# Scores and V of two units in every second turn, with V's last keys in column pairs

## The chip, the cores and the metric

The kernel runs on one core of a Trainium2 chip. A core has a matrix engine (TensorE) with its own weight loads, a vector engine (VectorE), a scalar engine (ScalarE), a general engine (GpSimd), and queues that issue transfers (here nearly all on SP). Each engine works through its own instructions in order; semaphores tie them together. The metric is the device time of one execution in microseconds, and fewer are better. Products land in PSUM[...]; everything else is in SBUF.

## The reference: what is computed

Two stages follow each other, all in fp32. The first is attention that keeps, for each query, the keys with the 32 highest scores. The second is a gated feed-forward block on the heads put side by side.

```
q, k, v: (8 batches, 8 heads, 576 positions, 64)
scores = (q @ k^T) / 8
kth    = the 32nd largest score of each query
scores = scores where scores >= kth, else -1e9
attn   = exp(scores - max);  attn = attn / (sum(attn) + 1e-9)
x      = (attn @ v), heads side by side: (4608 tokens, 512)
g      = x @ w_gate;  val = x @ w_val             (512 -> 1536)
out    = (g * sigmoid(g) * val) @ w_out           (1536 -> 512)
```

## The kernel before

**Units.** The attention is cut into 160 units, listed in `units`: for each batch, for each of five blocks of queries (`qt` 0 to 4), for each of four pairs of heads (`hp` 0 to 3). The first four query blocks have 128 queries; a unit of them handles both heads with 128 queries on the partitions. The fifth block (`qt == J`) has the last 64 queries, and its unit puts the two heads above each other on the partitions: "one-head" units, with half the work for VectorE. 576 keys are four chunks of 128 and a last one of 64.

**Steps of a unit.** `load` brings k and q in (six transfers on the queue of SP), `prep` transposes them on TensorE into a slab with the 64 features on the partitions, one head in each half. `scores` multiplies: each head uses one half of the rows, so the products are 64*128 tiles (64*64 for one-head units), in four PSUM banks (two), which ScalarE copies to `sc`. `select` finds the 32 highest per query on VectorE, in four rounds of the eight largest (line 328) and three replacements (line 332), and ends with a comparison (line 338). `penalize` adds on GpSimd (line 350). `weigh` takes exponentials and their sums on ScalarE (lines 359 and 364). `normalize` takes the reciprocal on VectorE (line 371) and scales on ScalarE (line 374). `turn` transposes the weights on TensorE (line 386) into `et`, copied by ScalarE (line 387). `values` multiplies V with `et`: for two-head units first the last 64 keys of both heads at once with `vlast`, a 128x128 block-diagonal weight (line 406), and then the four chunks of 128 keys with 64 columns for each head (line 415), which are 128*64 tiles: two heads side by side in the array's columns. For one-head units line 415 has chunks of 64 columns and then 64*64 tiles for the last keys. ScalarE copies the result to `xT` (line 430); where the unit's queries cross a border between blocks of 256 tokens, in two copies.

**Feed-forward.** `feed` does one block of 256 tokens in pieces, as soon as `xT` has all its heads: twelve gate and value products (line 470, full 128*128 tiles, eight instructions a piece), activations on ScalarE and products on GpSimd, and then the output product by seven quarters (line 556). A quantity `credit` meters how many pieces stand in a turn: `share` gives what VectorE's turn has room for, less what scores (0.7), V (0.7) and transposes (0.6) of that turn take on TensorE.

**Order.** The program is written out by hand, one turn per unit, and every engine keeps the order in which the instructions are issued. Turn n holds `select(n)` on VectorE, `penalize(n - 1)` on GpSimd, the scaling of unit n - 2, V of unit n - 3, the scores of unit n + 1, `weigh(n - 1)`, two feed-forward pieces, the transposes of unit n - 2, more pieces with `fetch(n + 2)` among them (which prepares a unit's slab, or issues the load for the next batch), and the reciprocal of unit n - 1 behind `select(n)`. The loads of units 2 and 3 are issued in turns 0 and 1.

**Buffers.** PSUM: five banks of tag `t` rotate through the kq transposes, scores, weight transposes and V; three of tag `f` serve the feed-forward part. SBUF: three buffers each for `sc` and `e`, two for `et` and for raw k and q, four for slabs and for V.

**Weights.** In the first turns the feed-forward weights are loaded and rounded, with work on ScalarE, VectorE and GpSimd (`rounded`, lines 106 to 123); `early` is the part of it that is issued between V and `weigh`.

Of the kernel before, what the change touches and what calls it, by code (L numbers as in the profile page):

```python
# [15 lines left out]
P = 128  # L16
# [9 lines left out]
def kernel(  # L26
# [370 lines left out]
    def values(n):  # L397

        b, qt, hp = units[n]
        vt, v_last, vl = vs[b * NHP + hp]  # L400
        et = state.pop(n)["et"]
        last = qt == J
        ql = R if last else P
        av = ps_t.tile([P, P], FP32, tag="t", name="av")
        if not last:
            nc.tensor.matmul(av[:], vl[:], et[:, J, :], start=True, stop=False)  # L406
        for c in range(J + 1 if last else J):
            kl = R if c == J else P
            for hh in range(2):
                moving = (  # L410
                    et[0:kl, c, hh * R : (hh + 1) * R]
                    if last
                    else et[:, c + hh * (J + 1), :]
                )
                nc.tensor.matmul(  # L415
                    av[hh * R : (hh + 1) * R, 0:ql],
                    v_last[:, hh, :] if c == J else vt[:, hh, c, :],
                    moving,
                    start=last and c == 0,
                    stop=c == (J if last else J - 1),  # L420
                )
        c0 = b * S + qt * P
        at = c0
        while at < c0 + ql:
            kb = at // BLK
            n_c = min((kb + 1) * BLK, c0 + ql) - at
            if kb not in xT:
# [3 lines left out]
                xT[kb][:, hp, at - kb * BLK : at - kb * BLK + n_c],  # L431
                av[:, at - c0 : at - c0 + n_c],
            )
            done[kb] += n_c
# [253 lines left out]
    def share(n):  # L688


        others = 0.0
        for m, cost in ((n + 1, 0.7), (n - TURN, 0.6), (n - VALUES, 0.7)):
            if m >= 0:
                others += cost * (0.5 if units[m][1] == J else 1)
        if units[n + 2][1] == 0:
            others += 0.6

        beside = 6.4 if T[1] else 7.0
        return beside * n_heads(units[n][1]) / 2 - others

# [9 lines left out]
    def finish_unit(n):  # L710
        values(n)
        b, qt, hp = units[n]
        if qt == J and b + 1 < B:
            load_v((b + 1) * NHP + hp)
# [7 lines left out]
    run(fetch(1))  # L722
    credit = [0.0]
    no = iter(())
    scaled = no
    TURN, VALUES = 2, 3
    due = [2.0]
    for n in range(NU + VALUES):
# [3 lines left out]
        nxt = scores(n + 1) if n + 1 < NU else no  # L732
        ahead = fetch(n + 2) if n + 2 < NU else no
# [19 lines left out]
        if n >= VALUES:  # L753
# [80 lines left out]
```

## Time and profile before

| what | value |
|---|---|
| median of three runs | 1810.51 us (1810.4 to 1811.54) |
| the profiled execution | 1810.53 us, of which 1808.5 us from first to last instruction |
| TensorE, products busy | 1703.6 us, 94% of the span |
| TensorE, weight loads busy | 1402.5 us, 78% |
| VectorE busy | 1615.7 us, 89% |
| ScalarE busy | 1221.0 us, 68% |
| GpSimd busy | 1039.2 us, 57% |
| DMA queue of SP and ScalarE | 57.37 MB, 12.3% of 16 engines' span |
| mean granted TensorE clock | 0.965 |

Busy time is the union of an engine's instructions in the profile. A matrix product is issued as two instructions, and consecutive ones overlap in the array; their ends are modelled, so the distance between starts says more than the durations. In the rows of the timeline an "x16" is a run of sixteen such instructions, with the time of the first start and the busy time of the run. A note in brackets is the idle time of the engine just before, and the instruction elsewhere that ended it. In the first 150 us TensorE is busy for 23 to 35 us of each 50 and its clock is granted at 0.59 to 0.73; from 350 us on it is at full clock nearly throughout.

### The profile page before, as it was taken

Reading aid. Unit: us, or ns where it says so; the run is one execution under the profiler, and the core shown is the slowest. Engines: PE = TensorE matmul, PEld = TensorE weight load, DVE = VectorE, ACT = ScalarE, POOL = GpSimd, SP = SyncE. Lnnn points to the kernel's source line nnn. Section 1 sums busy time; section 2 is a strip of 40 time slices with the busy share of each in tenths; the row PEclk is TensorE's granted clock in tenths of the full one; section 3 lists DMA queues with packets and bytes.
Section 4 is the critical chain, followed back from the end, with each engine's and each line's share of the span. In section 5 each row is a group of like instructions: output and inputs, shape, how many; then the busy total and the mean of one; then the engine's idle time right before and its main releaser. Section 6 shows DMA issues by size and latency. Waiting matters only on the chain.

```text
span 1808.5 us, 30379 instructions
## 1 busy us (share of the span) xinstructions
PE 1703.6 (94%) x10756; PEld 1402.5 (78%) x10756; DVE 1615.7 (89%) x3372; ACT 1221.0 (68%) x2977; POOL 1039.2 (57%) x930
## 2 busy tenths in 40 slices
PE   4559999799999999999999999999999999999999
PEld 2337678687888778887888878888888878888877
DVE  7999999999999999998999989998999979999400
ACT  7779676676767676767766776766776667676522
POOL 5778665455564646564555646655556544646434
PEclk7559999999999999999999999999999999999989
DMA  7433030002100030001200021000300011000000
GB/s 191 126 106 93 21 86 1 13 2 48 46 13 1 15 73 8 13 1 27 69 13 1 14 62 32 1 13 4 92 1 13 1 41 28 13 1 13 1 12 12
DMA packets 109304, 59.64 MB, mean 33 GB/s; under 512 B 88544, under 2 KB 96992, under 8 KB 109152
## 3 DMA queue, kind: packets, MB, share of 16 engines
q1 hardware_dynamic: 108016, 57.37, 12.3%
q8 instruction: 85, 1.39, 0.3%
q14 instruction: 67, 0.55, 0.1%
q10 hardware_dynamic: 1136, 0.33, 0.1%
HBM read 48.23 MB, written 9.44 MB: 32 GB/s over the span
## 4 chain that ended last, share of the span: by engine, by line
PE 83%; DVE 8%; ACT 6%; POOL 2%; issue 0%; DMA 0%; SPq 0%; ACTq 0%; POOLq 0%
PE f L470 40%; PE x_ps L556 9%; PE av L415 8%; PE s L308 7%; PE y_ps L556 7%; PE etps L386 6%; DVE m L328 3%; DVE e L332 3%; PE s L294 2%; PE av L406 2%; ACT et L387 1%; PE o_ps L516 1%; ACT e L359 1%; DVE e L338 1%; DVE size L121 1%; ACT kqT L268 1%
## 5 line engine op out<-in xcount | busy, mean ns | idle before, releaser
L328 DVE MAX8 m<-e 128x8 f32<-128x576 f32 x864 | 614.1, 746 | 3.3
L350 POOL TENSOR_TENSOR e<-e,sc 128x1152 f32<-128x1152 f32 (+1 forms) x160 | 383.0, 2394 | 86.1 <-DVE tot L371 70.1
L332 DVE MATCH_REPLACE8 e<-m,e 128x576 f32<-128x576 f32 x576 | 423.1, 740 | 0.0
L470 PE MATMUL f<-xT,wg 128*128 128x256 f32 x1728 | 406.5, 383 | 0.6 <-ACT xT L430 0.6
L470 PE MATMUL f<-xT,wv 128*128 128x256 f32 x1728 | 403.4, 382 | 0.0
L470 PEld LDWEIGHTS f<-xT,wg 128*128 128x128 f32 x1728 | 321.6, 191 | 61.0 <-issue 19.8
L470 PEld LDWEIGHTS f<-xT,wv 128*128 128x128 f32 x1728 | 320.6, 190 | 59.3 <-issue 19.7
L498 POOL TENSOR_TENSOR h<-h,half_g 128x512 f32<-128x512 f32 x108 | 137.7, 1275 | 285.5 <-ACT h L497 267.8
L503 POOL TENSOR_TENSOR h<-h,val 128x512 f32<-128x512 f32 x108 | 139.6, 1293 | 190.7 <-ACT val L502 190.4
L359 ACT ACTIVATE e<-e,bias 128x576 f32<-128x576 f32 x288 | 224.7, 795 | 26.7 <-POOL e L350 26.5
L374 ACT ACTIVATE e<-e,tot 128x576 f32<-128x576 f32 x288 | 210.1, 776 | 27.6 <-DVE tot L371 27.5
L387 ACT COPY et<-etps 128x512 f32<-128x512 f32 (+1 forms) x448 | 182.4, 480 | 53.6 <-PE etps L386 52.8
L332 DVE MATCH_REPLACE8 e<-m,sc 128x576 f32<-128x576 f32 x288 | 211.5, 739 | 0.0
L328 DVE MAX8 m<-sc 128x8 f32<-128x576 f32 x288 | 202.5, 738 | 9.3 <-ACT sc L313 9.3
L386 PE MATMUL etps<-ident,e 128*128 128x128 f32 (+1 forms) x1312 | 175.9, 279 | 18.7 <-ACT xT L430 12.7
L386 PEld LDWEIGHTS etps<-ident,e 128*128 128x128 f32 (+1 forms) x1312 | 155.9, 144 | 42.7 <-issue 25.2
L313 ACT COPY sc<-s 128x288 f32<-128x288 f32 x512 | 167.6, 417 | 26.5 <-PE s L308 25.3
L308 PE MATMUL s<-kqT 64*128 64x288 f32 x1024 | 170.3, 454 | 15.9 <-ACT kqT L268 15.1
L338 DVE TENSOR_SCALAR e<-sc,m 128x576 f32<-128x576 f32 x288 | 179.6, 659 | 1.1
L415 PE MATMUL av<-et,v 128*64 128x128 f32 (+1 forms) x2560 | 173.6, 280 | 6.9 <-ACT et L387 6.9
L415 PEld LDWEIGHTS av<-et,v 128*64 128x64 f32 x2560 | 136.4, 144 | 32.1 <-ACT et L387 9.3
L495 ACT ACTIVATE h<-f 128x512 f32<-128x512 f32 x108 | 64.1, 593 | 128.2 <-PE f L470 128.1
(73 smaller groups left out, 2038.8 us busy)
## 6 DMA issues: line engine op xcount, KB each, us to landing
v<-in_v_dram SPq DMA_DIRECT2D x32, 256.0 KB, 3.1
kq_in<-in_k_dram SPq DMA_DIRECT2D x63, 128.0 KB, 3.0
kq_in<-in_q_dram SPq DMA_DIRECT2D x63, 128.0 KB, 3.1
w<-in_moe_w_gate_dram SPq DMA_DIRECT2D x12, 512.0 KB, 3.8
w<-in_moe_w_val_dram SPq DMA_DIRECT2D x12, 512.0 KB, 3.8
w<-in_moe_w_out_dram SPq DMA_DIRECT2D x12, 512.0 KB, 3.6
out_dram<-o SPq DMA_DIRECT2D x38, 128.0 KB, 2.4
out_dram<-o SPq DMA_DIRECT2D x16, 256.0 KB, 2.4
```

What stands on the lines that cost most here:

```text
L308: nc.tensor.matmul(ps[:, 0:half], slab[d, q0 : q0 + P], slab[d, k0 : k0 + half])
L328: nc.vector.max(m[:, t, 8 * r : 8 * r + 8], cur[:, hs])
L332: nc.vector.match_replace(e[:, hs], m[:, t, 8 * r : 8 * r + 8], cur[:, hs], LOWEST)
L338: nc.vector.tensor_scalar(e[:, hs], sc[:, hs], m[:, t, TOP_K - 1 : TOP_K], FAR, ALU.is_lt, ALU.mult)
L350: nc.gpsimd.tensor_tensor(e[:, every], e[:, every], sc[:, every], ALU.add)
L359: nc.scalar.activation(e[:, hs], e[:, hs], AF.Exp, bias=bias[:, t : t + 1], scale=scale, accum_out=tot[:, t : t + 1],)
L374: nc.scalar.mul(e[:, hs], e[:, hs], tot[:, t : t + 1])
L386: nc.tensor.transpose(ps[0:kl, c * P : (c + 1) * P], e[:, k0 : k0 + kl], ident[:])
L387: nc.scalar.copy(et[0:kl, c0 : c0 + cn, :], ps[0:kl, 0 : cn * P].rearrange("p (c j) -> p c j", c=cn),)
L415: nc.tensor.matmul(av[hh * R : (hh + 1) * R, 0:ql], v_last[:, hh, :] if c == J else vt[:, hh, c, :], moving, start=last and c == 0, stop=c ...
L470: nc.tensor.matmul(ps[:, i, :], w[:, kc, m * P : (m + 1) * P], x[:, kc, :], start=(kc == 0), stop=(kc == KC - 1),)
L556: nc.tensor.matmul(ps, lhsT, T[i][m], start=m == 0, stop=m == MQ - 1)
```

## The change

Work is regrouped, and nothing of the result changes.

- In an even turn n the scores of units n + 1 and n + 2 are made, and V of units n - 4 and n - 3, in this order on TensorE: first scores, V of both, second scores. An odd turn has neither. The first turns (0 and 1) make one unit's scores each.
- On ScalarE the copies of the first scores stand before the V copy; the copies of the second scores stand behind `weigh(n - 1)`.
- The last 64 keys of a two-head unit go through two 128x64 halves of the same block-diagonal weight, as column tiles, in place of one 128x128 product.
- Both V results lie in one PSUM bank and are copied to `xT` by one instruction (two where a block border is crossed).
- `share` counts the costs in the turns in which they now fall. `fetch` runs one unit further ahead, and the loads of units 2 and 3 are issued before the first turn and in turn 0.

```diff
--- before.py
+++ after.py
@@ -394,33 +394,39 @@
 
     xT, done = {}, {}
 
-    def values(n):
-
-        b, qt, hp = units[n]
-        vt, v_last, vl = vs[b * NHP + hp]
-        et = state.pop(n)["et"]
+    def values(ns):
+
+        b, qt, hp0 = units[ns[0]]
         last = qt == J
         ql = R if last else P
-        av = ps_t.tile([P, P], FP32, tag="t", name="av")
-        if not last:
-            nc.tensor.matmul(av[:], vl[:], et[:, J, :], start=True, stop=False)
-        for c in range(J + 1 if last else J):
-            kl = R if c == J else P
-            for hh in range(2):
-                moving = (
-                    et[0:kl, c, hh * R : (hh + 1) * R]
-                    if last
-                    else et[:, c + hh * (J + 1), :]
-                )
-                nc.tensor.matmul(
-                    av[hh * R : (hh + 1) * R, 0:ql],
-                    v_last[:, hh, :] if c == J else vt[:, hh, c, :],
-                    moving,
-                    start=last and c == 0,
-                    stop=c == (J if last else J - 1),
-                )
+        av = ps_t.tile([P, 2, P], FP32, tag="t", name="av")
+        for i, n in enumerate(ns):
+            assert units[n] == (b, qt, hp0 + i)
+            vt, v_last, vl = vs[b * NHP + hp0 + i]
+            et = state.pop(n)["et"]
+            for c in (*range(J), J) if last else (J, *range(J)):
+                kl = R if last and c == J else P
+                for hh in range(2):
+                    d = slice(hh * R, (hh + 1) * R)
+                    if c == J:
+                        weights_, at = (v_last[:, hh, :], d) if last else (vl[:, d], None)
+                    else:
+                        weights_, at = vt[:, hh, c, :], d if last else None
+                    moving = (
+                        et[0:kl, c, at]
+                        if last
+                        else et[:, c + (0 if c == J else hh * (J + 1)), :]
+                    )
+                    nc.tensor.matmul(
+                        av[d, i, 0:ql],
+                        weights_,
+                        moving,
+                        start=c == (0 if last else J),
+                        stop=c == (J if last else J - 1),
+                    )
         c0 = b * S + qt * P
         at = c0
+        hps = slice(hp0, hp0 + len(ns))
         while at < c0 + ql:
             kb = at // BLK
             n_c = min((kb + 1) * BLK, c0 + ql) - at
@@ -428,10 +434,10 @@
                 xT[kb] = ffn.tile([P, NHP, BLK], FP32, tag="xT", name="xT", bufs=3)
                 done[kb] = 0
             nc.scalar.copy(
-                xT[kb][:, hp, at - kb * BLK : at - kb * BLK + n_c],
-                av[:, at - c0 : at - c0 + n_c],
+                xT[kb][:, hps, at - kb * BLK : at - kb * BLK + n_c],
+                av[:, 0 : len(ns), at - c0 : at - c0 + n_c],
             )
-            done[kb] += n_c
+            done[kb] += n_c * len(ns)
             at += n_c
 
     def store(o, g0, cols=slice(0, DM), queues=(nc.sync,)):
@@ -689,14 +695,25 @@
 
 
         others = 0.0
-        for m, cost in ((n + 1, 0.7), (n - TURN, 0.6), (n - VALUES, 0.7)):
+        costs = [(m, 0.7) for m in scored(n) + valued(n)] + [(n - TURN, 0.6)]
+        for m, cost in costs:
             if m >= 0:
                 others += cost * (0.5 if units[m][1] == J else 1)
-        if units[n + 2][1] == 0:
+        if units[n + 3][1] == 0:
             others += 0.6
 
         beside = 6.4 if T[1] else 7.0
         return beside * n_heads(units[n][1]) / 2 - others
+
+    def scored(n):
+
+        ahead = [n + 1] if n < 2 else [] if n % 2 else [n + 1, n + 2]
+        return [m for m in ahead if m < NU]
+
+    def valued(n):
+
+        behind = [] if n % 2 else [n - 4, n - 3]
+        return [m for m in behind if 0 <= m < NU]
 
     def pieces(n):
         for _ in range(n):
@@ -707,11 +724,12 @@
         for _ in steps:
             pass
 
-    def finish_unit(n):
-        values(n)
-        b, qt, hp = units[n]
-        if qt == J and b + 1 < B:
-            load_v((b + 1) * NHP + hp)
+    def finish_units(ns):
+        values(ns)
+        for n in ns:
+            b, qt, hp = units[n]
+            if qt == J and b + 1 < B:
+                load_v((b + 1) * NHP + hp)
 
     load(0)
     rounding(2)
@@ -720,17 +738,18 @@
     run(scores(0))
     early[0]()
     run(fetch(1))
+    load(2)
     credit = [0.0]
     no = iter(())
     scaled = no
-    TURN, VALUES = 2, 3
+    TURN = 2
     due = [2.0]
-    for n in range(NU + VALUES):
+    for n in range(NU + 3):
         nh = n_heads(units[n][1]) if n < NU else 1
         topk = select(n) if n < NU else no
         norm = normalize(n - 1) if 0 <= n - 1 < NU else no
-        nxt = scores(n + 1) if n + 1 < NU else no
-        ahead = fetch(n + 2) if n + 2 < NU else no
+        nxt = [scores(m) for m in scored(n)]
+        ahead = fetch(n + 3 if n else 2) if n + 3 < NU else no
 
         def dve(k, beside=True):
 
@@ -750,17 +769,24 @@
             penalize(n - 1)
         flush(on_pool)
         run(scaled)
-        if n >= VALUES:
-            finish_unit(n - VALUES)
-        run(nxt)
+        if nxt:
+            run(nxt.pop(0))
+        if valued(n):
+            finish_units(valued(n))
+        if nxt:
+            next(nxt[0])
         early[0]()
         if 0 <= n - 1 < NU:
             weigh(n - 1)
+        if nxt:
+            run(nxt.pop())
 
 
         dve(2, beside=False)
-        if 2 <= n + 2 < NHP:
-            load(n + 2)
+        if n == 0:
+            run(ahead)
+            load(3)
+            ahead = fetch(3)
         if n < NHP:
             load_v(n)
         pieces(2)
```

## The prediction

> **What bounds the kernel now.** I read the page first: TensorE's products are busy 1703.6 of 1808.5 us, its weight loads 1402.5, VectorE 1615.7, and the chain that ended last is 83% TensorE and 8% VectorE. The Trainium skill, "Perfetto Trace Analysis", Identifying the Most-Contended Engine, warns that busy time of products says little; so next the stages. One long window over the steady part, from 350 to 1650 us (columns: span, then busy time of TensorE, its loads, VectorE, ScalarE, GpSimd, then clock):
>
> ```profile
> 350.00:1650.00 1300.00, 1283.97 (x8338) 1071.43 (x8337) 1236.90 (x2601) 901.67 (x2235) 727.22 (x661) 1.00 0.09 22
> ```
>
> TensorE is idle 16.0 us of 1300, VectorE 63.1. Then TensorE's timeline through one turn (start, busy, instructions):
>
> ```profile
> 960.27 3.62 PE L470 MATMUL f<-xT,wv 128*128 128x256 f32 x16
> 963.73 0.38 PE L406 MATMUL av<-et,vlast 128*128 128x128 f32 x2
> 964.04 1.09 PE L415 MATMUL av<-et,v 128*64 128x128 f32 x16
> 965.07 1.24 PE L308 MATMUL s<-kqT 64*128 64x288 f32 x8
> 966.24 3.72 PE L470 MATMUL f<-xT,wg 128*128 128x256 f32 x16
> 969.79 1.15 PE L386 MATMUL etps<-ident,e 128*128 128x128 f32 x9
> ```
>
> There is no gap: every group starts where the one before ends. Only start-to-start times count, since ends are modelled. And VectorE at the end of that turn (in brackets the idle time and who ended it):
>
> ```profile
> 969.14 0.17 DVE L371 RECIPROCAL tot<-tot 128x2 f32<-128x2 f32 x1 [1.07 <-ACT tot L364]
> 970.98 0.09 DVE L332 MATCH_VALUE_LOAD e<-m,sc 128x8 f32 x1 [0.35 <-PE etps L386]
> ```
>
> VectorE waits for what follows TensorE. Taking the distance between reciprocals over the whole trace, an undisturbed two-head turn of VectorE is 10.56 us and a one-head turn 6.2 to 6.3; TensorE's turn is 10.5 with four feed-forward pieces and 12.2 with five; the five from 951.50 to 1008.34 average 11.37. From about 300 us on the time is TensorE's. Before that, and in the first 190 us above all, VectorE has no idle time and TensorE plenty: nothing is gained there. After the last softmax a whole feed-forward block (1743 to 1808 us) remains, which the change leaves alone. Where the 16 us of idle time sit: in the one-head turns at each batch's end, by the waits
>
> ```profile
> 1050.04 0.49 PE L406 MATMUL av<-et,vlast 128*128 128x128 f32 x2 [1.35 <-ACT et L387]
> ```
>
> **What the skill says.** "TensorEngine Tiling (Array Packing)", Key Properties: a change of tiling mode, not just of tile, drains the array. "TensorE: Matmul & The Clock Gate", Part 3, The mechanism: a weight load overlaps running products only where it goes to other rows. The trace agrees. A 256-column instruction goes every 0.216 us (3.46 for sixteen, 960.27 to 963.73), so 128 columns cost 0.108, and 288 columns 0.243. Pairs of column tiles and of row tiles run together. Over this, entering column tiles costs 0.31 - 2 x 0.108 = 0.10; entering row tiles 1.03 - 8 x 0.108 = 0.17; going back to the full array 1.17 - 4 x 0.243 = 0.20, and then 3.55 - 3.46 = 0.09 for the first loads. Going into the transposes costs nothing of this kind (nine in 0.99). So a turn pays 0.10 + 0.17 + 0.29 = 0.56 us for its three changes.
>
> **The change, part by part.**
> *Order on TensorE.* Two old turns pay 6 changes, 1.12 us. A new pair does scores, V of two units, scores: row tiles from the full array, columns from row tiles, row tiles, full array; the odd turn none. Two of these steps (full to row, row to column) are not in a full-clock stretch of the trace. If a step costs what its destination costs, they are 0.17 and 0.10; bounds are 0.09 each (a load hidden) and 0.29 each (the dearest step seen). Sum 0.17 + 0.10 + 0.17 + 0.29 = 0.73, so 0.39 saved per pair, between 0.08 and 0.48. I take the destination, because column tiles cost 0.10 both from the feed-forward part and from the kq transposes (four in 0.53).
> *Last keys in column pairs.* Two full instructions become four half-wide ones in two pairs: 2 x 0.108 both ways, so nothing; what it does is drop the line-406 group and its boundary, counted above.
> *How many.* 160 units, 80 pairs, of them 10 in the first batch, where VectorE bounds. Of the other 70, 56 are two-head: 56 x 0.39 = 22 us. In the 14 one-head pairs V itself goes from 128*64 to 64*64 tiles, twice now within a pair; 0.73 per turn before (0.10, 0.18, 0.15, 0.30 by the same reading), 1.18 for the pair after: 0.28 saved, 4 us.
> *One copy for both V results.* 192 copies (0.26 and 0.21 us) become 96 wider ones. ScalarE is busy 901.67 of 1300, so this is worth nothing by itself; its place matters. ScalarE in a pair turn runs: feed-forward items left over, scaling, four score copies, the V copy (which waits for both products), exponentials, the other four copies. With TensorE's turn start as zero, V ends at 0.17 + 0.97 + 0.10 + 20 x 0.108 = 3.4, the copy at 3.8, exponentials and their sums (2.0 + 0.3) at 6.1, the last copies at 7.4. Before, the sums were ready at about 5.3. VectorE's reciprocal waits for them, 0.8 us later, but in every second turn only; a VectorE pair is 21.1 us, TensorE's some 22.3, so the slack covers it. Without that slack it would be 0.8 x 56 = 45 us.
> *PSUM banks.* Five banks rotate: four scores, V, four scores. The second scores need the first banks copied out. In 16 of 109 two-head turns from 250 us on the scaling ended 3.1 us after V's start, as after 918 us, where line 374 ends at 921.38; copies then free two banks at 3.8 against 3.4. I charge 0.45 us to 15% of 60 pairs: 4 us lost.
> *V one turn later for even units, behind the first scores.* The last unit of a row keeps its turn, so feed-forward blocks come free when they did. V now has over 1 us more before it needs its transposed weights, and the odd turn has no V at all. Part of the 16 idle us should go: I take 4, bounds 0 and 16.
> *Transposes.* In pair turns they end at about 9.4 instead of 6.9 us after the start, in odd ones at 4.4. VectorE's first replacement of the next turn waits for them (the 0.35 above). That moves its phase by some 2 us, still within the pair's slack.
> *Loads and preparation a turn earlier.* Unit 3's load is six DMAs, about 0.64 us each on SP's queue, now ahead of V's four and the weights' in the first turn: 3.9 us. Behind them ScalarE's rounding waits (2.44 us on a weight piece already at 20.15); scores of unit 2 were copied by 26.2 for VectorE's use at 35.5, so the 9 us cover it; uncovered it would be 4. Later loads of line 221 wait for the same buffers one turn earlier, and stores behind them on SP are not waited for. The shares for pieces change from about 4.4 and 4.4 to 3.0 and 5.8: the same sum.
> *The end.* V of units 158 and 159 both stand after the last transposes; 158's runs while 159's weights are copied out: nothing.
>
> Sum: -22 - 4 + 4 - 4 = -26 us. The profiled execution took 1810.53 us for a span of 1808.5 (2.0 around it) and lies on the median, 1810.51. So 1810.5 - 26 = 1784.5.
>
> **Rivals.**
> *VectorE takes over (18%).* At 0.39 saved, TensorE's pair is 22.3 and VectorE's 21.1 plus GpSimd's hold on it: line 338 takes 0.93 or up to 1.96. For: whole rows of turns of 10.56 without idle time stand in the trace. Against: 63 idle us. If half the gain is lost, 1797.
> *One-head turns lose all their idle time and banks never stall (10%).* 26 + 12 + 4 = 42: 1768.
> *The unseen steps cost 0.29 each (5%).* 0.08 x 56 = 4, one-head pairs 2, stalls 4: about 1808, no change.
> *Slower (11%).* The second scores' copies stand behind the exponentials on ScalarE, and these wait for GpSimd (for line 350 in 17 places, 26.5 us in all). Their first bank is taken by the pair turn's second transpose at 4.9 + 3.46 + 0.43 = 8.8, and is free at 6.5: 2.3 us of room. With ScalarE later than that, each microsecond is TensorE's. It decides from 2.3 + 26/70 = 2.7 us late in every pair; at 3.0, 0.7 x 70 = 49 lost, 26 gained: 1833. Against: GpSimd is late in one turn of nine.
>
> **How the numbers follow.** The forecast has 56%. Faster are it and the first two rivals, 84%; within 0.2% (3.6 us, what a measurement of this kernel can just tell) 5%; slower 11%. The range runs from just below the second rival to the third, 1766 to 1808; the likeliest case alone spans 1775 to 1795.
>
> **What would show it.** Line 406's full-width rows gone; in the two-head pair turn, groups 64*128, 128*64 (forty), 64*128 with no gap, and starts 1.1, 2.3 and 1.2 us apart; TensorE's idle time from 350 us on below 16; VectorE's 61.5 us wait at line 620 unchanged, its idle time before that reduced. Wrong would be: first scores' or V's groups over 0.3 us longer than their columns, transposes waiting for ScalarE's score copies, or VectorE without idle time and TensorE with gaps.

## The result, and the profile after

| | before | after |
|---|---|---|
| median of the compared runs | 1810.58 us (4 runs, 1810.4 to 1811.54) | 1793.24 us (4 runs, 1792.28 to 1794.33) |
| the profiled execution, and its span | 1810.53, 1808.5 us | 1794.33, 1792.1 us |
| products, weight loads busy | 1703.6, 1402.5 us | 1691.1, 1398.6 us |
| VectorE, ScalarE, GpSimd busy | 1615.7, 1221.0, 1039.2 us | 1619.1, 1204.8, 1043.2 us |
| chain that ended last | 83% TensorE, 8% VectorE | 79% TensorE, 12% VectorE |

The ratio is 0.9903 [0.9886, 0.9921]: some 17 us gained, where 26 were forecast. The changed kernel took 1793.2 us against a predicted 1784.5.

First the long window of the prediction again, from 350 to 1650 us of the kernel after (span, then busy time of TensorE, its loads, VectorE, ScalarE and GpSimd, then the clock and DMA):

```profile
350.00:1650.00 1300.00, 1288.17 (x8656) 1079.44 (x8653) 1256.95 (x2641) 899.00 (x2187) 743.11 (x671) 1.00 0.09 22
```

TensorE's idle time fell from 16.0 to 11.8 us, VectorE's from 63.1 to 43.1. The count of products rose from 8338 to 8656; part of this is the last keys, which take twice as many instructions now, and the rest is more work done in the same stretch. VectorE's last wait, at the end of the program, is as long as before (62.1 us for 61.5), as forecast.

Then TensorE's timeline through the turn that the prediction showed, in the kernel after:

```profile
962.52 3.62 PE L476 MATMUL f<-xT,wv 128*128 128x256 f32 x16
966.06 1.24 PE L308 MATMUL s<-kqT 64*128 64x288 f32 x8
967.23 0.44 PE L420 MATMUL av<-et,vlast 128*64 128x128 f32 x4
967.50 1.04 PE L420 MATMUL av<-et,v 128*64 128x128 f32 x16
968.38 0.39 PE L420 MATMUL av<-et,vlast 128*64 128x128 f32 x4
968.59 1.04 PE L420 MATMUL av<-et,v 128*64 128x128 f32 x16
969.57 1.24 PE L308 MATMUL s<-kqT 64*128 64x288 f32 x8
970.74 2.86 PE L562 MATMUL y_ps<-wo,h 128*128 128x256 f32 x12
```

The order is scores, V of two units, scores, without a gap; the starts lie 1.17, 2.34 and 1.17 us apart, forecast 1.1, 2.3 and 1.2. The four products of last keys take 0.27 and 0.21 us from start to start (their columns: 0.22), so V is one block of 40 column products.

VectorE at the ends of turns in the kernel after (idle time and its releaser in brackets):

```profile
813.37 0.15 DVE L371 RECIPROCAL tot<-tot 128x2 f32<-128x2 f32 x1
815.87 0.09 DVE L332 MATCH_VALUE_LOAD e<-m,sc 128x8 f32 x1 [1.03 <-PE etps L386]
...
825.06 0.16 DVE L371 RECIPROCAL tot<-tot 128x2 f32<-128x2 f32 x1
...
834.66 0.17 DVE L371 RECIPROCAL tot<-tot 128x2 f32<-128x2 f32 x1 [3.19 <-ACT tot L364]
```

The wait for line 386 is still there, and at the reciprocals of a two-head pair (813.37, 825.06) VectorE no longer waits; the long wait for the sums (line 364) is behind a one-head unit. The waits of VectorE over 400 to 1650 us tell the same (total us, times, longest), before:

```profile
DVE tot L371 <- ACT tot L364: 37.0, 25, 6.7
DVE e L332 <- PE etps L386: 19.5, 26, 2.3
```

and after:

```profile
DVE tot L371 <- ACT tot L364: 18.8, 9, 4.7
DVE e L332 <- PE etps L386: 16.9, 16, 2.1
```

**Where the time went.** The reciprocal (line 371) comes once a turn, so its starts are a clock for VectorE. Start of the reciprocal of some units, before and after, in us:

| unit | before | after | difference |
|---|---|---|---|
| 0 | 35.5 | 37.2 | +1.8 |
| 8 | 135.2 | 136.9 | +1.8 |
| 14 | 213.4 | 216.8 | +3.4 |
| 24 | 304.2 | 310.0 | +5.8 |
| 33 | 400.6 | 405.5 | +4.9 |
| 159, the last | 1738.0 | 1720.9 | -17.1 |

By this clock the changed kernel is late by 4.9 us at unit 33 and gains 22.0 from there to the last unit. The three stages in windows, before:

```profile
0.00:200.00 200.00, 130.84 (x705) 98.02 (x707) 189.90 (x381) 160.15 (x360) 151.60 (x118) 0.74 0.44 120
200.00:400.00 200.00, 189.02 (x1210) 148.06 (x1205) 197.60 (x419) 137.63 (x346) 110.81 (x94) 0.98 0.09 25
400.00:1650.00 1250.00, 1233.97 (x8028) 1028.91 (x8028) 1186.90 (x2492) 864.40 (x2144) 702.40 (x641) 1.00 0.09 23
```

and after:

```profile
0.00:200.00 200.00, 126.77 (x703) 96.36 (x704) 188.05 (x375) 156.00 (x345) 147.72 (x115) 0.75 0.43 120
200.00:400.00 200.00, 189.52 (x1209) 148.11 (x1209) 197.24 (x417) 134.54 (x329) 112.15 (x95) 0.96 0.10 25
400.00:1650.00 1250.00, 1240.22 (x8358) 1038.86 (x8355) 1206.95 (x2532) 865.65 (x2109) 718.66 (x654) 1.00 0.09 23
```

In the first 200 us every engine is busy for less than before; after 400 us for more. Up to 400 us VectorE is busy for 387.5 and 385.3 of 400 us, and 9.3 and 9.2 of the rest is its very first wait for scores. Since it hardly waits otherwise, its lateness at unit 33 can be added up instruction by instruction, from start to start, over everything that it did until then:

| VectorE until the reciprocal of unit 33, us | before | after | |
|---|---|---|---|
| line 328, eight largest | 177.4 | 177.4 | 0 |
| line 332, replacements | 132.0 | 132.0 | 0 |
| line 121, rounding of weights, 36 instructions | 20.85 | 23.10 | +2.25 |
| line 338, comparison | 43.01 | 43.46 | +0.45 |
| waiting for line 114 (rounding on ScalarE) | 0 | 1.91 | +1.91 |
| waiting for line 386 (transposes) | 0 | 1.63 | +1.63 |
| waiting for line 364 (sums) | 1.16 | 0 | -1.16 |

The sum is +5.1, against 4.9 late; first waits and small instructions make up the rest. One row each for the two largest; VectorE after:

```profile
19.19 0.43 DVE L121 TENSOR_SCALAR size<-size 128x512 int32<-128x512 int32 x1 [1.91 <-ACT size L114]
...
152.30 2.75 DVE L121 TENSOR_SCALAR size<-size 128x512 int32<-128x512 int32 x1
```

and GpSimd after, in the time of the second row:

```profile
152.12 2.64 POOL L350 TENSOR_TENSOR e<-e,sc 128x1152 f32<-128x1152 f32 x1
154.72 1.48 POOL L509 TENSOR_TENSOR h<-h,val 128x512 f32<-128x512 f32 x1
```

The 36 instructions of line 121 have a median of 0.41 us. The one at 152.30 starts 0.18 us after GpSimd's line 350 and lasts until that has ended. Before, the longest took 1.48 us. Until unit 33 all instructions of lines 121 and 338 that took over 0.08 us longer than their short ones (33 before, 34 after) began while GpSimd worked, and of the short ones 27 of 69 and 22 of 68; what the long ones took over that adds up to 23.9 and 26.6 us, the 2.7 us of the table. The Trainium skill, "SBUF — State Buffer", Who interferes with whom, says that VectorE and GpSimd share a pair of ports, that the instruction which comes first holds it to its end, and that tensor_scalar can be one that needs it. The trace agrees, with 2.75 for 0.41 us here. The wait at 19.19 is that of the loads and the preparation issued earlier: on ScalarE the copies of unit 2's slab, at 17.25, now stand ahead of line 114, which began at 15.88 before and at 18.47 after.

VectorE's clock need not be TensorE's. For TensorE the columns that it has done can serve as a clock (0.216 us for 256, pairs of tiles counted once; 1557.8 us of columns in all, the same in both kernels). The changed kernel reaches what the kernel before had done at 180 us with a delay of 6.6 us, at 320 us with 3.3, and at 360 to 380 us with 8.2; at 1780 us it is 16.4 ahead, so by this clock it gains 24.6 from 380 us on. The step from 3.3 to 8.2 lies where TensorE has run out of feed-forward pieces and waits for others, ahead of the third feed-forward block, whose first piece starts before at

```profile
347.44 1.56 PE L470 MATMUL f<-xT,wg 128*128 128x256 f32 x6
```

and after at 357.19, behind the second scores of a pair:

```profile
354.69 2.57 PE L308 MATMUL s<-kqT 64*128 64x288 f32 x8 [2.04 <-ACT sc L313]
357.19 4.32 PE L476 MATMUL f<-xT,wg 128*128 128x256 f32 x16
```

The reciprocal that is due there, of unit 28, is 4.9 us late (352.7 for 347.8), the piece 9.8.

### The profile page after: what moved, and what is told of

Its sections match the earlier page's. It is cut to its first block, busy times and chain, and to the rows that moved or that the text cites. A ratio compares the mean times of both kernels' runs of the same rounds, so it can differ in the third digit from the quotient of the medians.

```text
span 1792.1 us, 30800 instructions
## 1 busy us (share of the span) xinstructions
PE 1691.1 (94%) x11012; PEld 1398.6 (78%) x11012; DVE 1619.1 (90%) x3372; ACT 1204.8 (67%) x2881; POOL 1043.2 (58%) x930
## 4 chain that ended last, share of the span: by engine, by line
PE 79%; DVE 12%; ACT 4%; POOL 3%; issue 1%; DMA 1%; SPq 0%; ACTq 0%; POOLq 0%; DVEq 0%
PE f L476 40%; PE x_ps L562 8%; PE av L420 8%; PE s L308 7%; PE etps L386 6%; PE y_ps L562 5%; DVE m L328 5%; DVE e L332 5%; PE s L294 2%; DVE e L338 1%; PE kqps L263 1%; PE o_ps L522 1%; ACT e L359 1%; POOL e L350 1%; DVE size L121 1%
## 5 line engine op out<-in xcount | busy, mean ns | idle before, releaser
L476 PEld LDWEIGHTS f<-xT,wg 128*128 128x128 f32 x1728 | 325.2, 192 | 52.0 <-issue 9.2
L359 ACT ACTIVATE e<-e,bias 128x576 f32<-128x576 f32 x288 | 221.9, 775 | 113.4 <-POOL e L350 113.3
L386 PE MATMUL etps<-ident,e 128*128 128x128 f32 (+1 forms) x1312 | 185.1, 284 | 48.1 <-ACT e L374 33.5
L374 ACT ACTIVATE e<-e,tot 128x576 f32<-128x576 f32 x288 | 210.7, 780 | 22.1 <-DVE tot L371 21.8
L308 PE MATMUL s<-kqT 64*128 64x288 f32 x1024 | 181.2, 461 | 37.3 <-ACT sc L313 22.0
L308 PEld LDWEIGHTS s<-kqT 64*128 64x128 f32 x1024 | 102.0, 198 | 85.2 <-ACT sc L313 27.3
L420 PE MATMUL av<-et,v 128*64 128x128 f32 (+1 forms) x2560 | 162.6, 271 | 0.0
L420 PEld LDWEIGHTS av<-et,v 128*64 128x64 f32 x2560 | 140.8, 143 | 7.2 <-issue 3.4
```

Source lines behind the costliest of these rows:

```text
L308: nc.tensor.matmul(ps[:, 0:half], slab[d, q0 : q0 + P], slab[d, k0 : k0 + half])
L359: nc.scalar.activation(e[:, hs], e[:, hs], AF.Exp, bias=bias[:, t : t + 1], scale=scale, accum_out=tot[:, t : t + 1],)
L374: nc.scalar.mul(e[:, hs], e[:, hs], tot[:, t : t + 1])
L386: nc.tensor.transpose(ps[0:kl, c * P : (c + 1) * P], e[:, k0 : k0 + kl], ident[:])
L420: nc.tensor.matmul(av[d, i, 0:ql], weights_, moving, start=c == (0 if last else J), stop=c == (J if last else J - 1),)
L476: nc.tensor.matmul(ps[:, i, :], w[:, kc, m * P : (m + 1) * P], x[:, kc, :], start=(kc == 0), stop=(kc == KC - 1),)
```

## The experiments

The two questions were whether the pieces of the sum are what the prediction took them for, and where the missing 9 us lie. Medians differ a little from chip to chip, so each run is given with its ratio to the kernel before on the same chip. "Excess" below is the start-to-start distance of a group less its columns at 0.216 us for 256, pairs of tiles counted once; values are medians over 400 to 1650 us.

**The old start.** Loads and preparation of units 2 and 3 are back in the turns where they were; the order of scores and V stays new.

```diff
-    load(2)
-        ahead = fetch(n + 3 if n else 2) if n + 3 < NU else no
+        ahead = fetch(n + (3 if n > 1 else 2)) if n + 3 < NU else no
-        if n == 0:
-            run(ahead)
-            load(3)
-            ahead = fetch(3)
+        if 2 <= n + 2 < NHP:
+            load(n + 2)
```

> The changed kernel, with the loads and preparations of units 2 and 3 back where the kernel before has them (the rest of the new order kept). Theory A, the start is what the forecast missed: VectorE's first rounding step waited 1.9 us in the changed kernel for ScalarE, which stood behind the earlier preparation and a later weight piece; by the 24th reciprocal the changed kernel is 5.75 us behind the kernel before. If all of it comes from the moved loads, this run is 4 to 6 us below the changed kernel, 1787.5 to 1789.5. Theory B, only the first 1.9 us come from there and the rest is chance of how GpSimd and VectorE meet in the first batch: 1791 to 1792. Theory C, the first batch's delay is made up for later anyway because TensorE bounds: no difference, 1793.

Measured: 1791.44 us (1789.49 to 1793.97), ratio 0.9900 [0.9887, 0.9914]. The 1.91 us wait is gone and the reciprocal of unit 1 starts at 47.2 instead of 48.7 us; that of unit 33 at 404.1 instead of 405.5. Over all profiles with full work on VectorE that reciprocal starts at 46.9 to 48.0 us in the four kernels with the old loads and at 48.1 to 48.9 in the six with the new ones. So the earlier loads cost some 1 us early on, where the prediction charged nothing; in the whole time it can't be told from the change as it is, whose interval it overlaps. Lines 121 and 338 together take 66.6 us until unit 33, as in the changed kernel: most of the lateness stays.

**Column pairs alone**, in the old order:

```diff
-            nc.tensor.matmul(av[:], vl[:], et[:, J, :], start=True, stop=False)
+            for hh in range(2):
+                d = slice(hh * R, (hh + 1) * R)
+                nc.tensor.matmul(av[d], vl[:, d], et[:, J, :], start=True, stop=False)
```

> The kernel before with one part of the change alone: the last 64 keys of V in two pairs of 64-column tiles instead of one full-width product. Theory A, as forecast: the same columns, the step into column tiles moves from behind the product to ahead of it, nothing is gained: 1810.6 within 1.5. Theory B, the boundary behind the full-width product (0.10 us) vanishes without a new one: 0.1 x 112 turns = 11 us less, 1799. In the changed kernel's trace the same group takes 0.27 instead of 0.31, which speaks for 0.04 x 112 = 4 us at most.

Measured: 1807.52 us, ratio 0.9994 [0.9986, 1.0002]. Nothing, as forecast: the old order leaves the full array in front of V either way, behind the last keys or ahead of them, and has three changes of mode in a turn with or without column pairs.

**The new order alone**, with full-width last keys:

```diff
-            for c in (*range(J), J) if last else (J, *range(J)):
+            if not last:
+                nc.tensor.matmul(av[:, i], vl[:], et[:, J, :], start=True, stop=False)
+            for c in (*range(J), J) if last else range(J):
```

> The changed kernel with the last 64 keys of V again in one full-width product per unit, so only the new order is left of the change. Theory A: the column pairs are worth something inside the new order, because a full-width product between column products is a change of tiling each way, twice in a pair: rows to full 0.29, into columns 0.10, back to full about 0.2, into columns 0.10, against 0.25 and 0.05 now; some 0.35 to 0.45 us in each of about 56 two-head pairs, 20 to 25 us: 1811 to 1817, the whole gain gone. Theory B, as a separate part it was worth nothing in the kernel before and is worth nothing here: 1792 to 1795.

Measured: 1817.38 us, ratio 1.0040 [1.0026, 1.0054]: slower than before. Its pair turn on TensorE:

```profile
933.54 1.24 PE L308 MATMUL s<-kqT 64*128 64x288 f32 x8
934.71 0.49 PE L408 MATMUL av<-et,vlast 128*128 128x128 f32 x2
935.13 1.09 PE L422 MATMUL av<-et,v 128*64 128x128 f32 x16
936.15 0.49 PE L408 MATMUL av<-et,vlast 128*128 128x128 f32 x2
936.57 1.09 PE L422 MATMUL av<-et,v 128*64 128x128 f32 x16
937.59 1.24 PE L308 MATMUL s<-kqT 64*128 64x288 f32 x8
938.76 3.72 PE L478 MATMUL f<-xT,wv 128*128 128x256 f32 x16
```

Two full products now take 0.42 us where their columns take 0.22, and the columns behind them 1.02 instead of 0.88. The excess of the pair is 1.31 us, against 0.76 in the changed kernel and 1.11 for two old turns. So 24 us of the changed kernel hang on the column pairs: they are nothing by themselves and everything inside the new order, because they are what keeps V of two units in one mode.

**Second scores behind two feed-forward pieces**, in turn 10 only, where TensorE stands still ahead of the first feed-forward block of the changed kernel, and then in every pair turn:

```diff
-        if nxt:
+        if nxt and not (n == 10):
             next(nxt[0])
 ...
         pieces(2)
+        if nxt:
+            run(nxt.pop())
```

> The changed kernel, with the second scores of one single turn (the tenth, in which the first feed-forward block becomes ready) moved behind the turn's first two feed-forward pieces. In the changed kernel's trace the second scores of this turn wait 4.53 us for ScalarE's copies of the first scores, and the first piece starts at 141.4 us instead of 135.7; TensorE has done 6.4 us less of its columns by 200 us. Theory A, this stall of the PSUM banks is the part of the forecast gain that is missing: the block starts some 5 us earlier and 4 to 6 us go, to 1787 to 1789. Theory B, TensorE only waits for VectorE elsewhere in the first batch (it has none of its idle time there): less than 1.5 us, 1792 to 1793.

The stall in question, in TensorE's timeline of the kernel after:

```profile
133.29 1.04 PE L420 MATMUL av<-et,v 128*64 128x128 f32 x16
138.87 2.58 PE L308 MATMUL s<-kqT 64*128 64x288 f32 x8 [4.53 <-ACT sc L313]
```

and what became of it with the second scores moved:

```profile
140.23 2.86 PE L476 MATMUL f<-xT,wg 128*128 128x256 f32 x12 [2.46 <-ACT xT L436]
```

Measured: 1792.89 us, ratio 0.9903 [0.9888, 0.9918]. The 4.53 us became 2.46 at the next group, waiting for the V copy, and nothing came of it in the end.

> The changed kernel, with the second scores of every pair turn behind the turn's first two feed-forward pieces. Theory A, the gain is the two changes of tiling saved per pair: this puts one group of row tiles by itself again (0.09 into it, 0.30 out of it, and 0.2 more for V into the full array, less 0.11 from V into rows), 0.4 to 0.5 us a pair, 25 to 32 us in 66 pairs, less 4 to 6 for the stall in the tenth turn: 1812 to 1820. Theory B, the gain comes from the looser order (V and copies having more time): most of it stays, 1788 to 1798.

Measured, with every pair turn so: 1805.42 us, ratio 0.9976 [0.9966, 0.9987]; 12 of the 17 us are given back. The second scores now stand between full groups and the excess of a pair rises from 0.764 to 0.923 us, 0.16 a pair. A rise of 0.4 to 0.5 was expected; leaving the full array once more costs only 0.09, and the transposes that now follow the second scores are 0.06 us over their usual time, where the first full product group of the changed kernel is 0.10 over.

**V ahead of both scores**, so that nothing covers the freeing of the banks:

```diff
-        if nxt:
-            run(nxt.pop(0))
         if valued(n):
             finish_units(valued(n))
+        if nxt:
+            run(nxt.pop(0))
```

> The changed kernel with V of both units ahead of both scores, so that a pair has three changes of tiling instead of four (full to columns, columns to rows, rows to full). Theory A, every change counts and the banks come free in time (ScalarE's copies start before the second scores' turn comes): 0.25 to 0.3 us a pair, 15 to 20 us less, 1773 to 1778. Theory B, the second scores then wait for the copies of the first, which V no longer covers: 0.3 to 1 us a pair is lost, and the sum is between 1793 and 1840. Theory C, VectorE bounds by now, so that at most 5 us go: 1788 to 1793.

Measured: 1799.41 us, ratio 0.9943 [0.9931, 0.9956]. One mode change fewer in every pair, and yet some 7 us slower than the changed kernel. TensorE's timeline shows where it goes:

```profile
926.55 2.67 PE L308 MATMUL s<-kqT 64*128 64x288 f32 x16
929.15 3.72 PE L476 MATMUL f<-xT,wv 128*128 128x256 f32 x16
```

Both scores together take 2.60 us for 1.94 of columns. The median excess is 0.577 where leaving this mode costs 0.198. The other 0.38 lie in the second half of the group, where in the turn shown pairs of products come 0.30 to 0.35 us apart instead of 0.24, while ScalarE copies out the banks of the first half: waits for a PSUM bank, by this pace and by the program (the profile names no releaser inside the group). With V between the two scores, as in the changed kernel, the second scores' median excess is 0.199, so V hides these copies.

**Old order in the first fourteen turns** (and the old loads with it), new from there:

```diff
-        ahead = [n + 1] if n < 2 else [] if n % 2 else [n + 1, n + 2]
+        ahead = [n + 1] if n < SINGLE else [] if n % 2 else [n + 1, n + 2]
-        behind = [] if n % 2 else [n - 4, n - 3]
+        behind = [n - 3] if n <= SINGLE else [] if n % 2 else [n - 4, n - 3]
```

with SINGLE = 14, and V ahead of the scores in those turns.

> The changed kernel, with the order of the kernel before (V of one unit, then scores of one, and the old loads) in the first 14 turns, and pairs from there on. In the changed kernel TensorE has done 6.4 us less of its columns by 200 us than in the kernel before, and neither the moved loads alone nor the second scores of turn 10 alone gave that back. Theory A, the loss comes from the pairs themselves while VectorE bounds and TensorE runs just behind it: in a pair turn V and its copy, and with them the first feed-forward block, wait for more of ScalarE. Then the columns by 200 us are those of the kernel before (91 to 92), and 5 to 7 us go: ratio to the kernel before 0.9865 to 0.9878, 1786.5 to 1789 where that takes 1810.5. Theory B, what is late in the first batch is made up by the wait around 330 us, where TensorE stands idle for VectorE and GpSimd in both kernels: less than 1.5 us, ratio 0.9895 to 0.9905.

Measured: 1794.38 us, ratio 0.9913 [0.9901, 0.9926]: nothing gained. Unit 14's reciprocal is at 214.4, only 1.0 late, but then the stall sits in the first pair turn, now before one-head scores:

```profile
193.57 1.19 PE L294 MATMUL s<-kqT 64*64 64x288 f32 x8 [3.70 <-ACT sc L313]
```

VectorE waits 2.5 us for sums behind it and unit 33 is at 406.1, later than in the changed kernel.

**Second scores' copies ahead of the exponentials** on ScalarE:

```diff
         if nxt:
-            next(nxt[0])
+            run(nxt.pop())
         early[0]()
 ...
             weigh(n - 1)
-        if nxt:
-            run(nxt.pop())
```

> The changed kernel, with ScalarE's copies of the second scores ahead of the exponentials instead of behind them. In the changed kernel the transposes of the weights, which use these banks next, start late: 7 us in all over 112 groups between 400 and 1650 us. Theory A, they wait for the banks: about 5 us go, ratio to the kernel before 0.987 to 0.9885, and the waits of the transposes for the score copies vanish. Theory B, the copies need the buffer that GpSimd's addition still reads, so exponentials and sums come later, VectorE waits for them: slower by 5 to 25 us, ratio 0.993 to 1.004. The forecast had neither: it put the loss of the banks, 4 us, on the second scores.

Measured: 1798.85 us, ratio 0.9939 [0.9927, 0.9951], slower than the changed kernel. The mean excess of the two-head transposes (98 groups) fell from 0.055 to 0.023 us, so these do wait for the banks of those copies. But VectorE waits longer for the sums (400 to 1650 us, this kernel):

```profile
DVE tot L371 <- ACT tot L364: 29.9, 15, 4.3
DVE e L332 <- PE etps L386: 5.8, 11, 0.9
```

29.9 us instead of 18.8. Theory B's number came; that these waits are what makes the kernel slower is likely and not shown. The place of the copies behind the exponentials is the better one.

**VectorE with less work.** The last of the four rounds of line 328 looks at half of the keys only, from the second batch on, in the kernel before and in the changed one:

```diff
+                hs_ = hs
+                if r == rounds - 1 and units[n][0] > 0:
+                    hs_ = slice(hs.start, hs.start + S // 2)
-                nc.vector.max(m[:, t, 8 * r : 8 * r + 8], cur[:, hs])
+                nc.vector.max(m[:, t, 8 * r : 8 * r + 8], cur[:, hs_])
```

> The kernel before, with VectorE lightened in all batches but the first: the fourth round's maximum reads only the first 288 of 576 keys of each head, so part of the selection is left out and more keys than 32 pass. It takes about 0.3 us off each head's turn, 0.6 of 10.56. If TensorE bounds the kernel before from about 400 us on, only the turns up to there (some 13) get shorter: 1801 to 1806, and VectorE's idle time grows by some 60 us. If VectorE bounded it, 0.6 x 112 + 0.3 x 28 = 76 us would go: 1735.

> The changed kernel with the same part of the selection left out in all batches but the first. Theory A, TensorE still bounds it: the same 5 to 9 us go as in the kernel before lightened alike, 1784 to 1788. Theory B, VectorE has taken over and ate the missing part of the forecast gain: another 5 to 15 us go on top, 1772 to 1780. The difference between the two lightened kernels is what the change is worth when VectorE is out of the way: 17 under A, 22 to 30 under B, against 26 forecast.

Measured: before, 1808.99 us, ratio 0.9996 [0.9988, 1.0004]; after, 1786.89 us, ratio 0.9875 [0.9860, 0.9891]. The kernel before doesn't answer to a lighter VectorE (5 to 9 us were expected), so from the second batch on its time is TensorE's, as the prediction read it. This holds although VectorE has hardly any idle time up to 400 us: its reciprocal of unit 33 now starts 4.2 us earlier (396.4 for 400.6), and TensorE's transposes of that unit only 1.3. The changed kernel becomes about 5 us faster, with the ends of the two intervals (0.9860 to 0.9891 and 0.9886 to 0.9921) overlapping, so these 5 us are likely rather than settled. There the reciprocal of unit 33 is 4.4 us earlier (401.1 for 405.5), and TensorE follows with 4.9. The transposes of unit 33 in the kernel before, and lightened:

```profile
409.09 1.15 PE L386 MATMUL etps<-ident,e 128*128 128x128 f32 x9
407.84 1.15 PE L389 MATMUL etps<-ident,e 128*128 128x128 f32 x9
```

and in the changed kernel, and lightened:

```profile
412.23 1.15 PE L386 MATMUL etps<-ident,e 128*128 128x128 f32 x9
407.36 1.15 PE L389 MATMUL etps<-ident,e 128*128 128x128 f32 x9
```

The gap between the two lightened kernels is 22.1 us.

The same in the first 36 units instead (`n < 36`):

> The kernel before, with VectorE lightened in the first 36 units alone: the fourth round's maximum reads the first 288 of 576 keys, so part of the selection is left out there. VectorE paces the start in both kernels, so both get faster; what counts is the difference to the changed kernel lightened alike. Here some 25 turns at 0.6 us bring the first feed-forward block forward: 8 to 18 us less, 1791 to 1801.

> The changed kernel lightened in the same way in the first 36 units. Theory A, the part of the forecast that is missing lies before 405 us, where VectorE is the pace and 4.9 us later than before by its 33rd reciprocal: then the gap between the two lightened kernels is 21 to 26 us instead of 17, with the turns behind them unchanged. Theory B, it lies behind 405 us, in single turns in which VectorE bounds: the gap stays at 16 to 19 us.

Measured: before, 1805.41 us, ratio 0.9972 [0.9963, 0.9981]; after, 1786.06 us, ratio 0.9869 [0.9855, 0.9882]. Both gain, which bears out that VectorE sets the pace somewhere in there, though the kernel before gains 5 us and not the 8 to 18 expected. The gap is 19.4 us, between the two theories; 17.3 was the gap of the full kernels, and the 2 us more are within the runs' spread. Unit 33's reciprocal is at 394.1 and 397.3, so the lateness shrank from 4.9 to 3.2 us only: VectorE's clock still runs behind, because lines 121 and 341 (which is 338 in the other kernels) together took 69.7 and 74.6 us, longer than with full work. TensorE's transposes of unit 33 are 3.6 us earlier in the kernel before and 8.7 in the changed one, for 6.6 and 8.2 us of VectorE: the changed kernel's TensorE follows VectorE through this stretch in full, that of the kernel before by half. From unit 33 on the changed kernel gains 19.4 + 3.2 = 22.6 us, by the same reckoning as the 22.0 of the full kernels.

## Why the prediction was right, and where it fell short

**The bound and the direction: right.** The kernel before is TensorE's from the second batch on (the lightened kernel before, 0.9996), and fewer mode changes shortened it.

**The order on TensorE: right, a little small in the saving.** Two old turns have an excess of 2 x 0.554 = 1.11 us (forecast 1.12), a pair now 0.764 (forecast 0.73): 0.344 saved instead of 0.39. The allocation of this sum was wrong. The prediction let each change cost what its destination costs. By group, in both kernels, it goes by the mode that is left: 0.09 to 0.10 out of the full array, to rows or to columns; 0.16 to 0.18 out of columns, to rows, to the full array or to 64*64 tiles; 0.20 out of rows of 64*128; and 0.10 more in the first full product group. An exception is the last transpose of a one-head unit, listed as a 128*64 tile: going into it and out of it costs under 0.01 us each. The skill's statement that a change of mode drains the array ("TensorEngine Tiling (Array Packing)", Key Properties), which the prediction cited, fits that reading better, since what drains is the work of the old mode; that this is the reason was not tested. The two allocations give nearly the same sum for the pair by luck. The prediction's other statement from the skill ("TensorE: Matmul & The Clock Gate", Part 3, The mechanism), that a weight load overlaps running products only where it goes to other rows, is not borne out by this trace: in its window of 1300 us products are busy for 1284 and loads for 1071, some 890 us of them loads of all 128 rows, so these run beside products too. The forecast's steps were read off the timeline and do not rest on it.

**From the reciprocal of unit 33 on: right in the sum.** By the prediction's terms that stretch holds 49 two-head pairs and 14 one-head pairs, (49 x 0.39 =) 19 + 4, plus 4 of idle time, less 4 of bank waits: 23 us. It gained 22.0. Of this, 49 x 0.344 = 17 is the two-head pairs. TensorE's idle time over 400 to 1650 us fell from 16.0 to 9.8, 6 us for a forecast of 4. The bank waits came mostly at another place than forecast: 1.7 us at the second scores (mean excess 0.255 against a median of 0.199 over 30 groups), and some 6 at the transposes behind them (two-head: 0.055 against 0.011 us over 98 groups, 4 us; one-head: 2 us). Transposes that wait for ScalarE's score copies were among the prediction's own signs of being wrong. In the one-head pairs, for which 4 us were forecast, the groups of 64*64 tiles lost some 5 us of excess (V's 4.0, the scores' 1.3). These terms overlap, since a wait can be idle time and excess, so they don't add up to the last us.

**Column pairs, the V copy and ScalarE's order: right.** Column pairs alone gave nothing (0.9994). The sums' lateness at line 364 is covered: VectorE's waits for it halved instead of growing. The slower rival, copies too late for the banks, did not come; moving them ahead made the kernel slower. What spoke against it was wrong, though: GpSimd is no longer late in one turn of nine, since ScalarE's exponentials now wait for line 350 in 59 places, 113.3 us in all, instead of 17 and 26.5.

**The step that failed: "nothing is gained there", and "the 9 us cover it".** The forecast lies 9 us off because the prediction took the start as neutral and counted savings from unit 20 on, about 239 us. At 380 to 400 us the changed kernel is late instead, by 4.9 us on VectorE's clock and 8.2 on TensorE's. Three terms were mis-sized:

1. VectorE was made slower by 4.9 us (5.1 when added up): 1.9 by the earlier loads and preparation (0.5 to 2.2 in the six profiles that have them, 0 to 0.2 in the four that have the old ones), 2.7 by being held longer by GpSimd at lines 121 and 338, and 0.5 by its waits for transposes less those for sums. The prediction checked whether the moved loads delayed the scores that VectorE needs 9 us later; it did not ask whether ScalarE's rounding, moved 2.6 us later by the same edit, has a VectorE instruction waiting behind it. Line 121 does.
2. Seven two-head pairs between unit 20 and unit 33 were counted at 0.39, 2.7 us. TensorE did catch up, from 6.6 to 3.3 us late between 180 and 320 us, but then it ran out of feed-forward pieces and had to wait for the late VectorE.
3. Bank waits were priced for full turns only. Where TensorE has run dry, as ahead of the first and the third feed-forward block, the block's first piece stands behind second scores that wait for the copies of the first (4.53 us in turn 10, 2.04 at 354.69), and the V copy that it needs stands behind the same copies on ScalarE. TensorE comes out of the second of these places 3.3 us later than VectorE's lateness accounts for. With the second scores moved behind the pieces the wait only changed its place: to 2.46 us for the V copy in turn 10 alone, and to 2.17 us at the third block (a start at 357.01) with every pair so.

On VectorE's clock 26 - 2.7 - 4.9 = 18.4, and with 22.0 in place of 23 for the rest, 17.4, against 17.1 between the last reciprocals and 16.4 between the spans; on TensorE's 24.6 - 8.2 = 16.4. Both sums close by construction: they locate the loss and don't prove its cause. That VectorE's time in the start reaches the end of the changed kernel is what its two lightened versions show; the third term's share stays open.

**The rival "VectorE takes over": partly true, in another place.** A lighter VectorE from the second batch on makes the changed kernel about 5 us faster and the old one not. The rival saw VectorE take over in the steady turns. But by columns TensorE is as late at 320 us in the lightened changed kernel as in the full one (3.4 and 3.3 us), and from 360 us on 3.3 instead of 8.2; at unit 91 the lead is 5.6 us (996.4 for 1002.0). So most of these 5 us come from the wait ahead of the third feed-forward block, before the steady stretch. (VectorE's clock hides this, since the two lightened kernels are 4.7 us apart at unit 33, as the full ones are.) The rival put it at half of the gain; it is about a fifth (5 of the 22 us between the lightened kernels). The runs' own spread of 2 to 3 us stands beside these differences.

**What stays open.** Why GpSimd's instructions meet line 121 and line 338 oftener in the new order. Until unit 33 these two take 66.1 to 67.6 us in the eight kernels of the new order with full work on VectorE, the one with old first turns at the lower end, and 63.9 and 64.9 in the two of the old order; each is one profile, and the step between the orders is hardly larger than the spread within one. Taking back the loads, the second scores of turn 10, or the pairs of the first fourteen turns changed the place of the delays and not their sum. Whether another order of the rounding work would free them was not tried.

## What to carry to other kernels

Count a regrouping on TensorE by changes of tiling mode, with each mode's exit price read from start-to-start distances, and remember that one product in another mode inside the group can cost the whole saving: here 24 us. Mark first in which stretch which engine sets the pace, and then ask of every edit what it does to that engine in that stretch. Being without idle time doesn't settle it: up to 400 us VectorE hardly waits in either kernel, yet a VectorE that was 4 us faster moved TensorE by 1.3 us in the one and by 4.9 in the other. Keep a clock for each engine, and look at the places where the engine that paces the rest runs dry. An order that puts other work between two groups sharing PSUM banks can be worth more than the mode change that it costs.

## What the runs showed of the hardware

- A change of tiling mode between groups of products costs by the mode left: 0.09 to 0.10 us out of 128*128, 0.16 to 0.18 out of 128*64, 0.20 out of 64*128, 0.15 out of 64*64, and 0.10 in the first full-width product group after it. A single transpose listed as 128*64 costs nothing of this kind.
- Four half-wide products in two column tiles take the time of two full-width ones (0.21 to 0.27 us for columns of 0.22): the tiling costs nothing as long as the mode stays.
- A VectorE tensor_scalar of 0.41 us took 2.75 us beside a GpSimd tensor_tensor of 2.64 us that had begun 0.18 us before it. Until unit 33 lines 121 and 338 took 66.6 instead of 63.9 us (one profile each), a larger loss than the wait that the moved loads caused.
- Weight loads of all 128 rows ran beside products: some 890 us of such loads and 1284 of products in 1300.
